# Score products of the first two batches in float32 from unsplit queries and keys

## The chip, the cores and the metric

The kernel runs on one core of one Trainium2 chip. The metric is device time in microseconds of one execution, lower is better. The core has TensorE (PE, with PEld for its weight loads), VectorE (DVE), ScalarE (ACT), GpSimd (POOL), and SyncE (SP), which here issues the transfers.

## The reference

Eight batches, eight heads, 576 positions, head width 64: block-causal attention (blocks of 64), then a feed-forward layer over all 4608 tokens.

```python
scores = scale * np.matmul(q, k.transpose(0, 1, 3, 2))
mask = block_i >= block_j
scores = np.where(mask, scores, -1000000000.0)
scores = scores - np.max(scores, axis=-1, keepdims=True)
attn = np.exp(scores)
attn = attn / (np.sum(attn, axis=-1, keepdims=True) + 1e-09)
out = np.matmul(attn, v)
...
h = x @ w_in
g = np.where(h >= 1, h, np.where(h <= -1, 0.0, (h + 1) ** 2 / 4))
return g @ w_out
```

All is float32, q and k of some size (standard deviation 0.8), so the products need more than one pass of a reduced format.

## The kernel before

Work goes by pairs of heads: 8 batches x 4 pairs = 32 pairs, the pairs of batch 0 first. `attention_steps` cuts each pair into eight steps and sets what the current pair, the next (its loads and turns) and the last (its product with the values) do in each. After 36 steps one step of `feed_forward` (twelve products of 512 columns) is written behind each attention step. Beside both runs `prepare_weights`, which splits the 64 pieces of the two weight matrices into high and low parts, by ACT, DVE, POOL, ACT and POOL in turn (L169 to L187), and has them done by about the end of batch 1. The framework then fixes each engine's order and the waits; each engine works strictly in that order.

A float32 product is made in one of two ways. *Split*: the operands become a high and a low part of type float32r, and the product is a sum of float32r matmuls. *Plain*: a matmul on float32 itself. Constants say which batches do what: `PLAIN = 2` (batches 0 and 1 multiply probabilities by values plainly), `RAW = 2` (from batch 2 on q and k are split after they are turned). In batches 0 and 1 q and k are split first: `split_q` (L351, L352) scales q and makes its parts on DVE; `split_k` makes k's high part on DVE (L363) and its low part on POOL (L364; for the very first pair on DVE).

The parts lie side by side, so that one turn (a matmul against the identity, L422) of a 128-token tile turns high and low at once: rows 0 to 63 one part, rows 64 to 127 the other. `turned` does four tiles of one head for q or k, copies the bank to `qb` or `kb` (L427, ACT), and has the upper or lower half moved to `qa` or `ka` by a transfer (L433; for the first head of the first pair by DVE, L429). `turned_last` does the same for the last 64 positions of both heads (L451, L456, L457).

`product` then makes a score tile of 128 queries from two float32r matmuls: L482 over `qa`, `ka` (68 rows: the high parts and four rows that hold the mask) and L485 over `qb`, `kb` (128 rows: the cross terms). `scores(j, g)` calls it for head j in three groups: tiles 0 and 1 (128 and 256 keys), tile 2 (384), tile 3 (512). `scores_last` takes the last 64 queries of both heads together as 128 columns, in two halves of 288 keys; `qa` and `qb` hold zeros beside each head's own 64 columns there, so the two heads' products are summed. After the product: maximum (L505, L529, DVE), exponential (L509, L535, ACT), reciprocal and scaling (L491, L492, L515, L541, DVE), turn of the probabilities (L554 in batch 0; in batch 1 by way of a transfer, L552), copy (L545, ACT), product with the values (L591). L541 runs once in a pair.

Of the kernel before, what the change touches and what calls it, by code (L numbers as in the profile page):

```python
# [8 lines left out]
F32 = mybir.dt.float32  # L9
# [3 lines left out]
AX = mybir.AxisListType  # L13
I32 = mybir.dt.int32
U32 = mybir.dt.uint32

# [7 lines left out]
def block_attn_then_ffn(  # L24
# [25 lines left out]
    G0 = 256  # L50
    G1 = S - G0
    SCALE = 1.0 / float(D) ** 0.5
# [39 lines left out]
    ident = ident_r.bitcast(F32)  # L92
# [28 lines left out]
    pcs = [const.tile([P, 2, BLK], F32R, tag=f"pcs{i}", name=f"pcs{i}") for i in range(2)]  # L121
# [16 lines left out]
    rows = mrow[:, :, :SM].rearrange("p s (t c) -> p s t c", c=P)  # L138
# [116 lines left out]
    class Pair:  # L255
# [4 lines left out]
        def __init__(self, b, hp):  # L260
            self.b, self.hp = b, hp

            self.plain = b < PLAIN
            self.first = b == 0 and hp == 0


            self.hop = b >= HOP
            self.raw = b >= RAW

            self.far = b >= FAR  # L270
            self.pr, self.nat = {}, {}
# [33 lines left out]
        def load(self, name):  # L305
            src = {"q": q, "k": k, "v": v}[name]
            h0 = 2 * self.hp
            if name == "v" and self.plain:

                self.vs = []  # L310
                both = att1.tile([P, 2, NTL + 1, 2, D], F32, tag="pb1", name="vs")
                for j in range(2):
                    vs = both[:, j]
                    nc.gpsimd.memset(vs[:, :, 1 - j, :], 0.0)
                    nc.sync.dma_start(
                        vs[:, :NTL, j, :], src[self.b, h0 + j, :SM, :].rearrange("(t p) d -> p t d", p=P)
                    )
                    nc.sync.dma_start(vs[:BLK, NTL, j, :], src[self.b, h0 + j, SM:, :])
                    self.vs.append(vs)
                return  # L320
            t_ = att2.tile([P, 2 * NTL + 2, D], F32, tag="nat", name=name + "n")
            if name == "v":
                for j in range(2):
                    nc.sync.dma_start(
                        t_[:, j * NTL : (j + 1) * NTL, :],
                        src[self.b, h0 + j, :SM, :].rearrange("(t p) d -> p t d", p=P),
                    )
                nc.sync.dma_start(
                    t_[:BLK, 2 * NTL :, :],
                    src[self.b, h0 : h0 + 2, SM:, :].rearrange("h p d -> p h d"),  # L330
                )
            else:

                nc.sync.dma_start(
                    t_[:, : 2 * NTL, :].rearrange("p (h t) d -> p h (t d)", h=2),
                    src[self.b, h0 : h0 + 2, :SM, :].rearrange("h (p t) d -> p h (t d)", t=NTL),
                )
                for j in range(2):
                    nc.sync.dma_start(
                        t_[j * BLK : (j + 1) * BLK, 2 * NTL, :], src[self.b, h0 + j, SM:, :]  # L340
                    )
            self.nat[name] = t_

        def split_q(self):
            if self.raw:
                return

            qn = self.nat.pop("q")[:, : 2 * NTL + 1, :]
            self.qs = att1.tile([P, 2 * NTL + 1, 2, D], F32R, tag="qs", name="qs")
            for c0, c1 in ((0, 2 * NTL), (2 * NTL, 2 * NTL + 1)):  # L350
                nc.vector.tensor_scalar_mul(self.qs[:, c0:c1, 0, :], qn[:, c0:c1, :], SCALE)  # L351
            nc.vector.scalar_tensor_tensor(  # L352
                out=self.qs[:, :, 1, :], in0=qn, scalar=SCALE,
                in1=self.qs[:, :, 0, :].bitcast(F32), op0=ALU.mult, op1=ALU.subtract,
            )

        def split_k(self):
            if self.raw:
                return
            kn = self.nat.pop("k")[:, : 2 * NTL + 1, :]  # L360
            self.ks = att1.tile([P, 2 * NTL + 1, 2, D], F32R, tag="ks", name="ks")
            for c0, c1 in ((0, 2 * NTL), (2 * NTL, 2 * NTL + 1)):
                nc.vector.tensor_copy(self.ks[:, c0:c1, 1, :], kn[:, c0:c1, :])  # L363
            (nc.vector if self.first else nc.gpsimd).tensor_tensor(  # L364
                out=self.ks[:, :, 0, :], in0=kn, in1=self.ks[:, :, 1, :].bitcast(F32),
                op=ALU.subtract,
            )
# [29 lines left out]
        def turned_raw(self, j):  # L397
# [10 lines left out]
            for a, bt, hi0 in ((qa, qb, 0), (ka, kb, D)):  # L408
                nc.sync.dma_start(
                    a[:D, j, :SM].bitcast(F32), bt[hi0 : hi0 + D, j, :SM].bitcast(F32)  # L410
                )

        def turned(self, is_q, j):

            if self.raw:
                if is_q:
                    self.turned_raw(j)
                return
            src, a, bt, hi0 = (self.qs, qa, qb, 0) if is_q else (self.ks, ka, kb, D)
            ps = work_bank("ps_qk")  # L420
            for t in range(NTL):
                nc.tensor.transpose(  # L422
                    ps[:, t * P : (t + 1) * P].bitcast(F32R), src[:, j * NTL + t, :, :], ident_r
                )

            turned = ps[:, :SM].rearrange("p (t c) -> p c t", t=NTL)
            nc.scalar.copy(bt[:, j, :SM].rearrange("p (c t) -> p c t", t=NTL), turned)  # L427
# [9 lines left out]
        def turned_last(self):  # L437

            ps = work_bank("ps_qk")
            if self.raw:  # L440
                ps = ps[:, :P]
                nc.tensor.transpose(ps.bitcast(F32R), self.qk[:, 2 * NTL, :, :], ident_r)
                ps = ps.rearrange("p (h c) -> p h c", h=2)
                self.parted(last_blocks, ps)
                for i, a in enumerate((qa, ka)):
                    nc.vector.tensor_scalar_mul(
                        last_blocks(a)[:D], ps[i * D : (i + 1) * D], 1.0 if i else SCALE
                    )
                return
            for i, src in enumerate((self.qs, self.ks)):  # L450
                nc.tensor.transpose(  # L451
                    ps[:, i * P : (i + 1) * P].bitcast(F32R), src[:, 2 * NTL, :, :], ident_r
                )
            for i, (a, bt, hi0) in enumerate(((qa, qb, 0), (ka, kb, D))):
                blocks = ps[:, i * P : (i + 1) * P].rearrange("p (h c) -> p h c", h=2)
                nc.scalar.copy(last_blocks(bt), blocks)  # L456
                nc.vector.tensor_copy(last_blocks(a)[:D], blocks[hi0 : hi0 + D])  # L457
# [14 lines left out]
        def begin_b(self):  # L472
            dt, n = (F32, 1) if self.plain else (F32R, 2)
            self.pb = [att1.tile([P, 2, NTL, G1], dt, tag=f"pb{i}", name=f"pb{i}") for i in range(n)]
            self.pc = (
                [att1.tile([BLK, 2, BLK], dt, tag="pa01", name="pc")] if self.plain else pcs
            )
            if not self.plain:
                self.x32 = att1.tile([P, S], F32, tag="x32", name="x32")

        def product(self, ps, j, c0, k0, n, first, last):
            nc.tensor.matmul(  # L482
                ps, qa[:KA, j, c0 : c0 + P], ka[:KA, j, k0 : k0 + n], start=first, stop=False
            )
# [400 lines left out]
```

## Time and profile before

| what | number |
|---|---|
| median of 3 runs | 1267.78 us (1264.84 to 1269.26) |
| profiled execution | 1269.69 us, span 1267.9 us |
| L541 (one in each pair) | first at 25.8 us, last at 1058.7 us |
| transfers, whole span | 215.43 MB, mean 170 GB/s |

Shares of the whole span mix three stages: batch 0 with attention alone, batch 1 with attention, feed-forward and the weights' split, and the rest. The prediction therefore reads the profile by stretches of the span.

### The profile page before, as it was taken

What the parts mean: (1) busy time and instruction counts of PE and PEld (TensorE: products, weight loads), DVE (VectorE), ACT (ScalarE), POOL (GpSimd) and SP (SyncE); (2) the same over time, 40 slices, a digit from 0 to 9 for tenths busy, and PEclk for the clock granted to TensorE, in tenths of its full rate; (3) what the DMA queues carried; (4) which work ended last, traced back from release to release, by engine and by line L of the source; (5) the groups of instructions that cost most, each with busy time, mean ns of one, the idle gap of its engine ahead of it and who ended that gap; (6) DMA issues with size and microseconds to landing.
All of it is one profiled execution on the core that took longest, in us unless ns stands there. A gap on an engine that the chain in (4) does not pass through costs nothing.

```text
span 1267.9 us, 20253 instructions
## 1 busy us (share of the span) xinstructions
PE 1200.1 (95%) x6280; PEld 998.8 (79%) x6280; DVE 887.0 (70%) x2188; ACT 703.2 (55%) x1827; POOL 394.6 (31%) x430
## 2 busy tenths in 40 slices
PE   5888889899999999999999999999999999999998
PEld 4666667678888888888888888888888888888886
DVE  8898877758777777777777777787777777322222
ACT  5787656646566655665656655566556555222222
POOL 3555655522222222222222222222222222222222
PEclk9888988999999999999999999999999999999999
DMA  5566666667888655555554655465556433422432
GB/s 158 167 176 215 203 228 197 217 198 237 260 273 266 215 162 158 154 175 163 156 162 145 187 157 152 138 189 153 160 154 190 137 128 118 132 87 98 133 100 100
DMA packets 185259, 215.43 MB, mean 170 GB/s; under 512 B 113840, under 2 KB 132272, under 8 KB 184384
## 3 DMA queue, kind: packets, MB, share of 16 engines
q1 hardware_dynamic: 185152, 214.14, 54.9%
q8 instruction: 50, 0.82, 0.3%
q14 instruction: 57, 0.47, 0.1%
HBM read 134.74 MB, written 31.98 MB: 131 GB/s over the span
## 4 chain that ended last, share of the span: by engine, by line
PE 69%; DVE 16%; ACT 6%; issue 5%; DMA 1%; POOL 1%; SPq 1%; ACTq 0%; POOLq 0%; DVEq 0%
PE ph L770 29%; PE po L794 15%; PE po L799 7%; PE ps_av L591 7%; PE ps_s L482 4%; ACT pr L509 3%; PE ps_s L485 3%; DVE t L780 2%; PE ps_t L552 2%; DVE t L783 2%; ACT t L779 2%; DVE pb L547 2%; DVE nm L505 2%; DVE sm L491 1%; DVE pr L515 1%
## 5 line engine op out<-in xcount | busy, mean ns | idle before, releaser
L785 POOL TENSOR_TENSOR gl<-t,gh 128x512 fp32r<-128x512 f32 x144 | 187.5, 1302 | 510.2 <-ACT gh L784 333.2
L794 PE MATMUL po<-wo,gh 128*128 128x512 f32 x1152 | 296.1, 397 | 0.5 <-DMA wo<-wo_split 0.3
L794 PEld LDWEIGHTS po<-wo,gh 128*128 128x128 f32 x1152 | 212.5, 189 | 44.5 <-DMA wo<-wo_split 0.7
L770 PE MATMUL ph<-xh,wih 128*128 128x512 f32 x576 | 232.9, 404 | 1.6 <-DVE t L783 1.6
L770 PE MATMUL ph<-xh,wil 128*128 128x512 f32 x576 | 228.8, 397 | 0.0
L770 PE MATMUL ph<-xl,wih 128*128 128x512 f32 x576 | 227.8, 396 | 0.5 <-DVE xl L627 0.5
L780 DVE SCALAR_TENSOR_TENSOR t<-t 128x512 f32<-128x512 f32 x144 | 101.5, 705 | 168.0 <-ACT t L779 165.2
L779 ACT ACTIVATE t<-ph 128x512 f32<-128x512 f32 x144 | 85.9, 597 | 173.8 <-PE ph L770 173.8
L509 ACT ACTIVATE pr<-ps_s,nm 128x128 f32<-128x128 f32 (+3 forms) x256 | 134.1, 527 | 60.5 <-DVE nm L505 58.4
L784 ACT CAST gh<-t 128x512 fp32r<-128x512 f32 x144 | 89.5, 621 | 120.3 <-DVE t L783 120.0
L799 PE MATMUL po<-wo,gl 128*128 128x512 f32 x576 | 155.6, 392 | 0.0
L482 PE MATMUL ps_s<-ka,qa 68*128 68x288 f32 (+4 forms) x384 | 135.3, 367 | 15.0 <-ACT pr L509 5.4
L379 POOL TENSOR_TENSOR vsr<-vn,vsr 128x256 fp32r<-128x256 f32 (+1 forms) x96 | 55.2, 576 | 246.2 <-ACT vsr L378 244.6
L770 PEld LDWEIGHTS ph<-xh,wil 128*128 128x128 f32 x576 | 109.5, 190 | 23.8
L770 PEld LDWEIGHTS ph<-xh,wih 128*128 128x128 f32 x576 | 109.8, 191 | 21.7 <-DVE t L783 2.3
L799 PEld LDWEIGHTS po<-wo,gl 128*128 128x128 f32 x576 | 108.7, 189 | 23.1
L505 DVE TENSOR_REDUCE nm<-ps_s 128x1 f32<-128x128 f32 (+3 forms) x256 | 118.8, 482 | 10.4 <-PE ps_s L485 9.4
L770 PEld LDWEIGHTS ph<-xl,wih 128*128 128x128 f32 x576 | 109.7, 190 | 20.5 <-DVE xl L627 0.9
L485 PE MATMUL ps_s<-kb,qb 128*128 128x288 f32 (+4 forms) x384 | 121.1, 322 | 0.0
L515 DVE TENSOR_SCALAR pr<-pr,sm 128x128 f32<-128x128 f32 (+3 forms) x256 | 107.3, 440 | 5.4
L783 DVE TENSOR_TENSOR t<-ph,t 128x512 f32<-128x512 f32 x144 | 98.7, 686 | 2.2
L491 DVE TENSOR_SCALAR sm<-sm 128x1 f32<-128x1 f32 (+1 forms) x224 | 52.0, 232 | 68.3 <-ACT pr L509 65.7
(111 smaller groups left out, 1871.4 us busy)
## 6 DMA issues: line engine op xcount, KB each, us to landing
wo<-wo_split SPq DMA_DIRECT2D x144, 512.0 KB, 3.5
prr<-pr SPq DMA_DIRECT2D x96, 192.0 KB, 2.5
prr<-pr SPq DMA_DIRECT2D x72, 256.0 KB, 2.8
out_dram<-ob SPq DMA_DIRECT2D x36, 256.0 KB, 2.9
bits<-in_moe_w_in_dram SPq DMA_DIRECT2D x32, 256.0 KB, 3.5
bits<-in_moe_w_out_dram SPq DMA_DIRECT2D x32, 256.0 KB, 3.0
wo_split<-ws SPq DMA_DIRECT2D x16, 512.0 KB, 2.9
qa<-qb SPq DMA_DIRECT2D x63, 128.0 KB, 2.4
```

Source lines behind the costliest of these rows:

```text
L482: nc.tensor.matmul(ps, qa[:KA, j, c0 : c0 + P], ka[:KA, j, k0 : k0 + n], start=first, stop=False)
L485: nc.tensor.matmul(ps, qb[:, j, c0 : c0 + P], kb[:, j, k0 : k0 + n], start=False, stop=last)
L505: nc.vector.tensor_reduce(out=nm[:, i : i + 1], in_=ps[:, cs], axis=AX.X, op=ALU.max, negate=True)
L509: nc.scalar.activation(pr[:, cs], ps[:, cs], AF.Exp, bias=nm[:, i : i + 1], scale=1.0, accum_out=sm[:, i : i + 1],)
L515: nc.vector.tensor_scalar_mul(pr[:, cs], pr[:, cs], sm[:, i : i + 1])
L770: nc.tensor.matmul(ph, w[:, cc, fs], x[:, cc, xs], start=(cc == 0 and i == 0), stop=(cc == NCC - 1 and i == 2),)
L779: nc.scalar.activation(t_, ph, AF.Relu, bias=0.5, scale=0.5)
L780: nc.vector.scalar_tensor_tensor(out=t_, in0=t_, scalar=1.0, in1=t_, op0=ALU.min, op1=ALU.mult)
L783: nc.vector.tensor_tensor(out=t_, in0=ph, in1=t_, op=ALU.max)
L785: nc.gpsimd.tensor_tensor(out=gl, in0=t_, in1=gh.bitcast(F32), op=ALU.subtract)
L794: nc.tensor.matmul(po[tt], gh[:, ts_], wo[:, w, :], start=(fc == 0 and w == 0), stop=False)
L799: nc.tensor.matmul(po[tt], gl[:, ts_], wo[:, 0, :], start=False, stop=fc == NFC - 1)
```

## The change

`UNSPLIT = 2`: the pairs of batches 0 and 1 skip `split_q` and `split_k`. The two heads' q (or k) are loaded so that tile t holds both heads' 64 numbers side by side, and `turned_unsplit` turns four such tiles (float32) for both heads at once: head 0 in rows 0 to 63, head 1 in rows 64 to 127. One ACT instruction copies the bank out (with the scale, for q) into a tile `qkt` that holds turned q and k of a pair; two buffers alternate. `turned_last_unsplit` turns the last blocks and writes q's to the diagonal of `diag`, a 128x128 part of a constant tile `corner` that is zero beside its two blocks.

`product` becomes, for a tile of one head, one float32 matmul over that head's 64 rows, and one float32r matmul over the four mask rows (rows 64 to 67 of `qa` and `ka`), which touches only the last 128 columns. For the last block it is one float32 matmul over 128 rows for both heads. A float32 matmul stands once in the order and runs as two instructions on PE.

```diff
+    UNSPLIT = 2
+    corner = att1.tile([P, G0 + P], F32, tag="pa01", name="corner")
+    nc.vector.memset(corner[:, P:], 0.0)
...
         def split_q(self):
-            if self.raw:
+            if self.raw or self.unsplit:
                 return
...
+        def turned_unsplit(self, is_q):
+            if is_q:
+                tag = ("qs", "ks")[self.hp % 2]
+                both = att1.tile([P, 2, S], F32, tag=tag, name="qkt")
+                self.qt, self.kt = both[:, 0, :], both[:, 1, :]
+                self.diag = corner[:, (1 + self.hp % 2) * P :][:, :P]
+            src = self.nat["q" if is_q else "k"]
+            ps = work_bank("ps_qk")
+            for t in range(NTL):
+                nc.tensor.transpose(ps[:, t * P : (t + 1) * P], src[:, 2 * t : 2 * t + 2, :], ident)
+            nc.scalar.mul(
+                (self.qt if is_q else self.kt)[:, :SM].rearrange("p (c t) -> p c t", t=NTL),
+                ps[:, :SM].rearrange("p (t c) -> p c t", t=NTL), SCALE if is_q else 1.0,
+            )
+
+        def turned_last_unsplit(self):
+            ps = work_bank("ps_qk")
+            for i, name in enumerate("qk"):
+                nc.tensor.transpose(
+                    ps[:, i * BLK : (i + 1) * BLK], self.nat.pop(name)[:BLK, 2 * NTL :, :],
+                    ident[:BLK, :BLK],
+                )
+            for j in range(2):
+                rows = slice(j * D, (j + 1) * D)
+                nc.scalar.mul(self.diag[rows, rows], ps[rows, :BLK], SCALE)
+            nc.scalar.copy(self.kt[:, SM:S], ps[:, BLK : 2 * BLK])
...
         def product(self, ps, j, c0, k0, n, first, last):
+            if self.unsplit and c0 == SM:
+                if j == 0:
+                    nc.tensor.matmul(ps, self.diag, self.kt[:, k0 : k0 + n], start=True, stop=True)
+                return
+            if self.unsplit:
+                rows = slice(j * D, (j + 1) * D)
+                nc.tensor.matmul(
+                    ps, self.qt[rows, c0 : c0 + P], self.kt[rows, k0 : k0 + n],
+                    start=first, stop=False,
+                )
+                nc.tensor.matmul(
+                    ps[:, n - P :], qa[D:KA, j, c0 : c0 + P], ka[D:KA, j, c0 : c0 + P],
+                    start=False, stop=last,
+                )
+                return
```

What it does to the order of the engines. PE in batch 1, head 1's first two groups; before, each tile is two float32r products, with a turn of the next pair's keys between:

```order
L482 MATMUL ps_s<-ka,qa 128x128
L485 MATMUL ps_s<-kb,qb 128x128
L482 MATMUL ps_s<-ka,qa 128x256
L485 MATMUL ps_s<-kb,qb 128x256
L422 MATMUL ps_qk<-ident_r,ks 128x128 x4
L552 MATMUL ps_t<-ident_r,vsr_111 128x128 x4
L794 MATMUL po<-wo,gh 128x512 x8
L799 MATMUL po<-wo,gl 128x512 x4
L482 MATMUL ps_s<-ka,qa 128x384
L485 MATMUL ps_s<-kb,qb 128x384
```

The same place after the change (L544 is the float32 product over 64 rows, L548 the mask product over four):

```order
L544 MATMUL ps_s<-qkt 128x128
L548 MATMUL ps_s<-ka,qa 128x128
L544 MATMUL ps_s<-qkt 128x256
L548 MATMUL ps_s<-ka,qa 128x128
L623 MATMUL ps_t<-ident_r,vsr_111 128x128 x4
L865 MATMUL po<-wo,gh 128x512 x8
L870 MATMUL po<-wo,gl 128x512 x4
L544 MATMUL ps_s<-qkt 128x384
L548 MATMUL ps_s<-ka,qa 128x128
```

Product and mask now alternate, and the second turn of the keys is gone. DVE at the same pair, before: the split of the next pair's q and k stands among the scaling of the probabilities.

```order
L505 TENSOR_REDUCE nm<-ps_s 128x1
L351 TENSOR_SCALAR qs<-qn 128x8x64
L491 TENSOR_SCALAR sm<-sm 128x2
L351 TENSOR_SCALAR qs<-qn 128x64
L492 RECIPROCAL sm<-sm 128x2
L363 CAST ks<-kn 128x8x64
L515 TENSOR_SCALAR pr<-pr,sm 128x128
L515 TENSOR_SCALAR pr<-pr,sm 128x256
L491 TENSOR_SCALAR sm<-sm 128x1
L457 CAST qa<-ps_qk 64x2x64
L492 RECIPROCAL sm<-sm 128x1
L352 SCALAR_TENSOR_TENSOR qs<-qn,qs 128x9x64
```

After (L562, L563 and L586 are the old L491, L492 and L515; L576 is L505, and L177 to L183 are the weights' split):

```order
L562 TENSOR_SCALAR sm<-sm 128x2
L563 RECIPROCAL sm<-sm 128x2
L586 TENSOR_SCALAR pr<-pr,sm 128x128
L586 TENSOR_SCALAR pr<-pr,sm 128x256
L576 TENSOR_REDUCE nm<-ps_s 128x1
L177 TENSOR_SCALAR work<-work 128x256
L180 TENSOR_SCALAR work<-work 128x256
L183 SCALAR_TENSOR_TENSOR work<-work 128x256
L562 TENSOR_SCALAR sm<-sm 128x1
L563 RECIPROCAL sm<-sm 128x1
```

The five instructions of the split and the copy of the last block are gone from between. On PE the last block's products, before:

```order
L482 MATMUL ps_s<-ka,qa 128x288
L485 MATMUL ps_s<-kb,qb 128x288
L482 MATMUL ps_s<-ka,qa 128x288
L485 MATMUL ps_s<-kb,qb 128x288
L482 MATMUL ps_s<-ka,qa 128x288
L485 MATMUL ps_s<-kb,qb 128x288
L482 MATMUL ps_s<-ka,qa 128x288
L485 MATMUL ps_s<-kb,qb 128x288
L552 MATMUL ps_t<-ident_r,prs 128x128 x3
```

After, with the work around it:

```order
L544 MATMUL ps_s<-qkt 128x512
L548 MATMUL ps_s<-ka,qa 128x128
L623 MATMUL ps_t<-ident_r,vsr_112 128x128 x3
L865 MATMUL po<-wo,gh 128x512 x8
L870 MATMUL po<-wo,gl 128x512 x4
L540 MATMUL ps_s<-qkt,corner 128x288 x2
L623 MATMUL ps_t<-ident_r,prs 128x128 x3
```

Eight products became two.

More of the change, by code (lines that the diff above doesn't have):

```diff
@@ L332, in load @@
             else:
[L334 to L338, printed above, removed]
+                if self.unsplit:
+                    for j in range(2):
+                        nc.sync.dma_start(
+                            t_[:, j : 2 * NTL : 2, :],
+                            src[self.b, h0 + j, :SM, :].rearrange("(p t) d -> p t d", t=NTL),
+                        )
+                else:
                     nc.sync.dma_start(
-                        t_[j * BLK : (j + 1) * BLK, 2 * NTL, :], src[self.b, h0 + j, SM:, :]
-                    )
+                        t_[:, : 2 * NTL, :].rearrange("p (h t) d -> p h (t d)", h=2),
+                        src[self.b, h0 : h0 + 2, :SM, :].rearrange("h (p t) d -> p h (t d)", t=NTL),
+                    )
+                if self.unsplit:
+                    nc.sync.dma_start(
+                        t_[:BLK, 2 * NTL :, :],
+                        src[self.b, h0 : h0 + 2, SM:, :].rearrange("h p d -> p h d"),
+                    )
+                else:
+                    for j in range(2):
+                        nc.sync.dma_start(
+                            t_[j * BLK : (j + 1) * BLK, 2 * NTL, :], src[self.b, h0 + j, SM:, :]
+                        )
             self.nat[name] = t_
         def split_q(self):
-            if self.raw:
+            if self.raw or self.unsplit:
                 return
@@ L411, in turned_raw @@
                 )
+        def turned_unsplit(self, is_q):
[18 more added lines that the diff above has]
+                    ident[:BLK, :BLK],
+                )
+            for j in range(2):
+                rows = slice(j * D, (j + 1) * D)
+                nc.scalar.mul(self.diag[rows, rows], ps[rows, :BLK], SCALE)
+            nc.scalar.copy(self.kt[:, SM:S], ps[:, BLK : 2 * BLK])
         def turned(self, is_q, j):
+            if self.unsplit:
+                if j == 0:
+                    self.turned_unsplit(is_q)
+                return
             if self.raw:
@@ L437, in turned_last @@
         def turned_last(self):
+            if self.unsplit:
+                self.turned_last_unsplit()
+                return
             ps = work_bank("ps_qk")
@@ L475, in begin_b @@
             self.pc = (
-                [att1.tile([BLK, 2, BLK], dt, tag="pa01", name="pc")] if self.plain else pcs
+                [corner[:BLK, :P].rearrange("p (h c) -> p h c", h=2)] if self.plain else pcs
             )
```

9 lines of the change are left out of this document (8 added, 1 removed).

## The prediction

> **What bounds the kernel now.** First the first part of the page, then the table of windows, cut where the change's eight pairs (batches 0 and 1) begin and end. The columns after the length are busy microseconds, with instruction counts in brackets; then come the granted TensorE clock, the DMA share and GB/s.
>
> ```profile
> PE 1200.1 (95%) x6280; PEld 998.8 (79%) x6280; DVE 887.0 (70%) x2188; ACT 703.2 (55%) x1827; POOL 394.6 (31%) x430
> 0.00:25.80 25.80, 12.36 (x54) 10.14 (x54) 21.22 (x67) 14.16 (x41) 9.54 (x18) 1.00 0.57 159
> 25.80:114.60 88.80, 72.96 (x390) 58.65 (x391) 80.14 (x250) 69.78 (x213) 46.81 (x60) 0.90 0.61 179
> 114.60:290.10 175.50, 156.16 (x730) 121.87 (x729) 127.19 (x309) 101.93 (x284) 85.12 (x102) 0.92 0.67 211
> 25.80:290.10 264.30, 229.12 (x1119) 180.51 (x1120) 207.33 (x558) 171.71 (x496) 131.93 (x161) 0.92 0.65 201
> 290.10:323.30 33.20, 32.80 (x184) 27.70 (x183) 26.42 (x65) 20.87 (x54) 9.14 (x10) 1.00 0.70 211
> ```
>
> The cuts are the starts of the L541 instruction, one in each pair. From 290 us on PE is busy 32.80 of 33.20 us and nothing there is changed: that stage only shifts. From 25.8 to 114.6 (batch 0) VectorE is busy 80.14 of 88.80 us and PE 72.96; from 114.6 to 290.1 (batch 1 with the first feed-forward steps) PE is busy 156.16 of 175.50 and VectorE 127.19. So before 290 us there are two near-bounds, VectorE first and then PE, and the change moves work from the one to the other. PE is idle 264.30 - 229.12 = 35.2 us in the two stages together. What ends that idle time stands in the waits of that stretch (total, times, longest):
>
> ```profile
> PE ps_t L554 <- DVE sm L491: 7.5, 3, 3.8
> PE ps_s L482 <- ACT kb L427: 4.1, 2, 3.7
> PE ps_av L591 <- ACT pr L509: 3.7, 3, 2.2
> PE ps_t L554 <- DVE pr L515: 3.4, 4, 1.5
> PE ph L770 <- DVE t L783: 1.6, 3, 0.7
> ```
>
> Of the 35.2 us, 7.5 + 3.4 + 1.6 = 12.5 us end with VectorE and 4.1 us with the copy of keys that the change replaces: 16.6 us that lighter VectorE and ScalarE queues could return. The rest ends with exponentials, transfers and copies that stay.
>
> **The change, part by part.** Instructions that go, with mean ns in the same stretch:
>
> ```profile
> L364 POOL TENSOR_TENSOR ks<-kn,ks 128x576 fp32r<-128x576 f32 x6 | 8.6, 1435 | 0.6 <-DVE ks L363 0.3
> L427 ACT CAST kb<-ps_qk 128x512 fp32r<-128x512 f32 x14 | 8.2, 585 | 0.0
> L352 DVE SCALAR_TENSOR_TENSOR qs<-qn,qs 128x576 fp32r<-128x576 f32 x6 | 4.4, 739 | 0.0
> L363 DVE CAST ks<-kn 128x512 fp32r<-128x512 f32 x6 | 3.3, 551 | 0.0
> L351 DVE TENSOR_SCALAR qs<-qn 128x512 fp32r<-128x512 f32 x6 | 2.9, 480 | 0.0
> L363 DVE CAST ks<-kn 128x64 fp32r<-128x64 f32 x6 | 2.5, 409 | 1.2 <-DMA kn<-in_k_dram 1.2
> L457 DVE CAST ka<-ps_qk 64x128 fp32r<-64x128 f32 x7 | 2.1, 293 | 0.2
> L351 DVE TENSOR_SCALAR qs<-qn 128x64 fp32r<-128x64 f32 x6 | 2.0, 338 | 0.0
> L457 DVE CAST qa<-ps_qk 64x128 fp32r<-64x128 f32 x7 | 1.9, 272 | 0.0
> L456 ACT CAST qb<-ps_qk 128x128 fp32r<-128x128 f32 x7 | 1.9, 272 | 0.0
> ```
>
> VectorE loses 739 + 551 + 480 + 409 + 293 + 338 + 272 = 3082 ns a pair. POOL loses 1.4 us a pair. ScalarE goes from four wide copies and two of the last block (4 x 585 + 2 x 272 = 2.9 us) to two wide and three of the last block (2 x 585 + 3 x at most 272 = 2.0 us): 0.9 us less, nothing of it on PE's own path beyond the 4.1 us of waiting above. Four transfers a pair go; the loads are cut in other pieces:
>
> ```profile
> ka<-kb SPq DMA_DIRECT2D x63, 128.0 KB, 2.3
> qn<-in_q_dram SPq DMA_DIRECT2D x8, 256.0 KB, 3.5
> vs<-in_v_dram SPq DMA_DIRECT2D x16, 128.0 KB, 2.3
> ```
>
> A query or key load of 256 KB (3.5 us to landing) becomes two of 128 KB in 64-number pieces, the form of the value load, which lands in 2.3 us; the issues of a pair stay six, since the two last-block loads become one. They are issued a pair ahead, so I cost them at nothing; what covers them is that pair's 20 us. If a key load waits for its buffer, now held until the last block is turned, the transfers queued behind it on SP wait too: bound 0 to 2.3 us a pair, taken 0 because the last block is turned two steps before the next load is issued.
>
> PE pays. Its price per column comes from the order of time (start, length, group), batch 0's second pair and the end of batch 1:
>
> ```profile
> 33.26 0.31 PE L482 MATMUL ps_s<-ka,qa 68*128 68x128 f32 x1
> ...
> 33.80 0.60 PE L554 MATMUL ps_t<-ident_r,pr 128*128 128x128 f32 x4
> 34.15 0.42 PE L482 MATMUL ps_s<-ka,qa 68*128 68x384 f32 x1
> ...
> 34.59 0.23 PE L451 MATMUL ps_qk<-ident_r,qs 128*128 128x128 f32 x1
> ...
> 39.68 0.50 PE L482 MATMUL ps_s<-ka,qa 68*128 68x512 f32 x1
> ...
> 40.25 0.49 PE L554 MATMUL ps_t<-ident_r,pr 128*128 128x128 f32 x3
> ...
> 41.58 0.40 PE L482 MATMUL ps_s<-ka,qa 68*128 68x288 f32 x1 [0.27 <-DVE ka L457]
> ...
> 42.22 0.49 PE L554 MATMUL ps_t<-ident_r,pr 128*128 128x128 f32 x3
> 43.57 0.54 PE L422 MATMUL ps_qk<-ident_r,qs 128*128 128x128 f32 x4 [0.40 <-DVE xl L627]
> 43.95 0.46 PE L770 MATMUL ph<-xh,wih 128*128 128x512 f32 x1
> ...
> 277.30 0.43 PE L591 MATMUL ps_av<-pc,vs 64*128 64x64 f32 x2
> 277.66 2.21 PE L591 MATMUL ps_av<-pb,vs 128*128 128x320 f32 x8
> 279.80 0.43 PE L591 MATMUL ps_av<-pc,vs 64*128 64x64 f32 x2
> ```
>
> Products before, by distances of starts: 0.54 + 0.44 + 0.57 us for a head's three groups, and 0.64 us for four products of the last block, of which there are eight: 2 x 1.55 + 2 x 0.64 = 4.4 us a pair.
>
> A float32 product is two instructions on PE (the L591 group shows eight for four matmuls). From 277.66 to 279.80, 6 x 320 + 2 x 192 = 2304 columns and one change of rows (128 to 64) take 2.14 us; from 277.30 to 277.66, 2 x 64 columns and one change back take 0.36 us. Solved: 0.82 ns a column and 0.25 us a change of rows. The turns of L554, 0.11 us each within their group of four, say 0.86 ns a column and then 0.16 us a change. I take 0.82 ns and 0.20 us.
>
> After: 2 x 1280 + 2 x 288 = 3136 columns, twice 0.82 ns each, is 5.1 us; eight mask products of 128 columns, at the 0.64 us / (4 x 288) = 0.56 ns a column of the last block's old products, add 0.6 us. That is 5.7, so +1.3 us. Turns: sixteen at 0.095 us (0.38 us for four at 43.57) become eight at 0.11: -0.6 us.
>
> Changes of rows have no counterpart in the old products, all of which use 68 or 128 rows. Now a group goes 128 rows, 64 (product), 4 (mask), and for the first group 64 and 4 once more: 5 + 3 + 3 = 11 a head, 22 a pair, and one at the turn of the last block: 23. For head 0 the product uses rows 0 to 63 and the mask rows 64 to 67, so five of the 23 are between rows that do not overlap; the trace shows no such pair. I count half of them: 20.5, about 4.0 us at 0.20 us. The ends are none at all (0) and 23 x 0.25 = 5.75 us.
>
> The Trainium skill has a rule for either end. "TensorEngine Tiling (Array Packing)", Key Properties, says that a change of tiling mode drains the engine, which would charge all 23 (about 0.5 us a pair more than I take, +4 us in all); "TensorE: Matmul & The Clock Gate", Step-by-step, says that weights load ahead of a running matmul where the row groups do not conflict, which would charge 18 (-4 us in all). The row at 277.30 bears out the first for overlapping rows; no row decides for disjoint ones.
>
> PE in sum: +1.3 - 0.6 + 4.0 = +4.7 us a pair (ends +0.7 and +6.4). Between 25.8 and 290 us lie seven and a half pairs' scores: +35 us (ends +5 and +48). Against it:
> - Idle of PE: VectorE sheds 7.5 x 3.08 = 23 us, more than the 16.6 us of waits found above. I take 16 (ends 5 and 23).
> - Clock: 0.92 granted over 264.30 us is 21 us lost at most; the loss follows idle stretches, and PE grows denser. I take half, 10 (ends 0 and 18).
> - Start: the first pair's split and copy by VectorE go, of which these two rows lie on the chain of waits,
>
> ```profile
> 9.19 3.02 DMA ka<-mrow
> 22.23 1.28 DVE qs L352
> ```
>
> while the mask rows (landing at 12.21 us) are still needed, one memset more (of the new constant tile) heads VectorE's queue, and PE has more to do. I take -2 (ends -4 and +3).
>
> 35 - 16 - 10 - 2 = +7 us. The profiled execution took 1269.69 us (span 1267.9), 1.9 above the median of the runs shown, 1267.78; the forecast goes from the median: 1275.
>
> **Rivals.** *The clock returns more.* Denser PE work keeps the full clock nearly throughout, 18 us instead of 10: -1, so 1267. For it: 0.90 and 0.92 granted against 1.00 after 290 us. Against it: the waits on L509 remain, and they make the idle stretches. The same page's Part 1 says that idle windows of about 3.4 us halve the clock and busy ones restore it.
>
> *Faster.* The changes of rows are hidden and VectorE was the true bound: +5 - 12 - 2 = -9, so 1259. It decides if a product followed by its mask takes less than 0.1 us beyond its columns. Against it: the 0.36 us for two 64-column instructions.
>
> *PE takes it all.* Idle time comes from the softmax's own latency and stays: 35 - 5 - 3 = +27, so 1295. For it: PE 156.16 of 175.50 in batch 1.
>
> **How the numbers follow.** Forecast 0.40, clock 0.25, faster 0.23, PE takes it all 0.12. Slower by over 0.3% (3.8 us, about what a measurement tells from no change) is 0.52, within 0.25, faster 0.23. The range, 1258 to 1292, cuts the far parts of the second and third rival; the forecast's own range is 1271 to 1283.
>
> **What would show it.** Right: VectorE some 3 us a pair lighter before 290 us, the score products at about 9 to 10 us of PE a pair, about 0.2 us from each product's end to its mask, fewer waits on VectorE, pairs of batch 1 no shorter, and 33.2 us a pair unchanged afterwards. Wrong: a mask product that follows its product at once, a shorter batch 0, or a granted clock near 1.00 before 290 us.

## Result and the profile after

| | before | changed |
|---|---|---|
| median | 1267.16 us (1264.84 to 1269.26, 4 runs) | 1284.29 us (1281.31 to 1288.57, 4 runs) |
| profiled execution | 1269.69 us, span 1267.9 | 1283.15 us, span 1281.4 |

The ratio is 1.0138, with an interval of 1.0118 to 1.0158: slower, by 17 us where +7 was forecast. The new number is inside the range given, but not inside the forecast's own range of 1271 to 1283. The two profiled executions differ by 13.5 us; the rest lies between single executions, and no profile shows it.

The first part of the page and the table of windows of the changed kernel, cut as before at the start of the instruction that opens each pair (L541 is now L612). The columns are busy microseconds of PE, PEld, DVE, ACT and POOL with counts, then granted clock, DMA share, GB/s:

```profile
PE 1239.4 (97%) x6248; PEld 999.7 (78%) x6248; DVE 865.6 (68%) x2130; ACT 699.3 (55%) x1819; POOL 379.6 (30%) x423
0.00:27.70 27.70, 18.93 (x49) 10.64 (x49) 14.48 (x52) 13.09 (x39) 6.96 (x17) 1.00 0.54 147
27.70:130.30 102.60, 96.83 (x366) 62.08 (x367) 74.18 (x227) 68.19 (x212) 38.69 (x58) 0.82 0.55 164
130.30:303.50 173.20, 165.05 (x728) 118.80 (x727) 119.08 (x290) 100.75 (x280) 80.44 (x98) 0.97 0.71 225
27.70:303.50 275.80, 261.88 (x1092) 180.88 (x1093) 193.26 (x516) 168.93 (x490) 119.14 (x155) 0.91 0.65 202
303.50:336.70 33.20, 32.84 (x185) 27.76 (x183) 26.45 (x66) 20.87 (x54) 9.16 (x10) 1.00 0.87 279
```

The start grew by 1.9 us (25.8 to 27.7), batch 0 from 88.8 to 102.6 us (+13.8), batch 1 went from 175.5 to 173.2 (-2.3), and a later pair still takes 33.20 us. In sum +13.4 us, which is the difference of the two profiled executions (13.5). So the loss sits in batch 0. There PE's busy time went from 72.96 to 96.83 us while its granted clock (the share of full speed that TensorE is allowed) fell, by the rows, from 0.90 to 0.82. VectorE, near-bound before, is busy 74.18 of 102.60 us.

PE's idle time in both batches is 275.80 - 261.88 = 13.9 us, where it was 35.2. Its largest waits there (total, times, longest):

```profile
PE ps_av L662 <- ACT pr L580: 4.0, 3, 2.3
PE ps_t L625 <- DVE pr L586: 3.7, 2, 2.1
PE ps_qk L444 <- ACT pb L616: 2.4, 2, 2.0
PE ps_t L625 <- ACT pr L580: 1.6, 1, 1.6
```

The 7.5 us on VectorE's `sm` and the 4.1 us on the copy of keys are gone.

**A blind spot of the clock column.** The profile's record of the clock begins at 32.8 us in the kernel before and at 26.5 us in the changed one; ahead of it the column prints 1.00. The spacing of the products says otherwise. The same five turns of the probabilities, kernel before (at 26.40 us), then changed (at 28.79 us):

```profile
26.40 1.30 PE L554 MATMUL ps_t<-ident_r,pr 128*128 128x128 f32 x5 [2.08 <-DVE sm L491]
```

```profile
28.79 0.74 PE L625 MATMUL ps_t<-ident_r,pr 128*128 128x128 f32 x5 [1.61 <-ACT pr L580]
```

They start 0.213 us apart in the first and 0.109 us apart in the second. So the kernel before runs at half clock from its start until 32.8 us, 7.0 us of which belong to batch 0, and the 1.00 of both kernels' first row is no measurement. With those 7.0 us counted, batch 0's clock before the change is 0.86, not 0.90. In what follows half clock is counted with them.

What the forecast had not seen is in the windows at half clock. First two rows of the changed kernel's batch 0, then one of the kernel before:

```profile
29.90:47.00 17.10, 17.10 (x43) 10.42 (x42) 10.27 (x32) 10.28 (x33) 5.88 (x8) 0.50 0.37 117
77.70:87.90 10.20, 10.20 (x32) 6.51 (x31) 5.07 (x19) 6.05 (x18) 0.73 (x1) 0.50 0.42 117
```

```profile
49.80:56.60 6.80, 6.24 (x26) 5.47 (x26) 6.07 (x19) 3.72 (x10) 4.07 (x5) 0.50 0.54 149
```

Before, no recorded stretch at half clock was longer than 6.8 us. After the change one lasts 17.1 us and two last 10.2, and in them PE is busy 17.10 of 17.10 and 10.20 of 10.20 us. In batch 0 half clock covers 37.5 us instead of 24.0; in batch 1 it is 10 us instead of 27. One profile is not exact here: in three traces of the kernel before (two with streams appended behind it, below) batch 0 has 22.5, 24.0 and 25.7 us, and both batches together 43, 51 and 59.

### The profile page after: what moved, and what is told of

Its sections match the earlier page's. It is cut to its first block, busy times and chain, and to the rows that moved or that the text cites. A ratio compares the mean times of both kernels' runs of the same rounds, so it can differ in the third digit from the quotient of the medians.

```text
span 1281.4 us, 20013 instructions
## 1 busy us (share of the span) xinstructions
PE 1239.4 (97%) x6248; PEld 999.7 (78%) x6248; DVE 865.6 (68%) x2130; ACT 699.3 (55%) x1819; POOL 379.6 (30%) x423
## 4 chain that ended last, share of the span: by engine, by line
PE 65%; DVE 9%; ACT 4%; issue 3%; POOL 0%; ACTq 0%; POOLq 0%
PE ph L841 27%; PE po L865 15%; PE po L870 7%; PE ps_av L662 6%; PE ps_s L553 3%; ACT pr L580 3%; PE ps_s L556 2%; PE ps_t L623 2%; DVE t L851 2%; DVE pb L618 2%; DVE t L854 2%; ACT t L850 2%; DVE sm L562 1%; PE ps_qk L421 1%; DVE x L685 1%
## 5 line engine op out<-in xcount | busy, mean ns | idle before, releaser
L841 PE MATMUL ph<-xh,wil 128*128 128x512 f32 x576 | 226.2, 393 | 0.0
L576 DVE TENSOR_REDUCE nm<-ps_s 128x1 f32<-128x128 f32 (+3 forms) x256 | 118.8, 482 | 24.2 <-PE ps_s L548 21.0
L399 POOL TENSOR_TENSOR vsr<-vn,vsr 64x64 fp32r<-64x64 f32 (+1 forms) x96 | 55.6, 579 | 249.2 <-ACT vsr L398 247.6
L586 DVE TENSOR_SCALAR pr<-pr,sm 128x128 f32<-128x128 f32 (+3 forms) x256 | 103.8, 426 | 6.3 <-DVE sm L563 0.3
L562 DVE TENSOR_SCALAR sm<-sm 128x1 f32<-128x1 f32 (+1 forms) x224 | 52.7, 235 | 79.6 <-ACT pr L580 76.7
L553 PE MATMUL ps_s<-ka,qa 68*128 68x288 f32 (+4 forms) x288 | 99.4, 360 | 5.3 <-ACT pr L580 5.3
L556 PE MATMUL ps_s<-kb,qb 128*128 128x288 f32 (+4 forms) x288 | 88.7, 315 | 0.0
```

What stands on the lines that cost most here:

```text
L553: nc.tensor.matmul(ps, qa[:KA, j, c0 : c0 + P], ka[:KA, j, k0 : k0 + n], start=first, stop=False)
L556: nc.tensor.matmul(ps, qb[:, j, c0 : c0 + P], kb[:, j, k0 : k0 + n], start=False, stop=last)
L576: nc.vector.tensor_reduce(out=nm[:, i : i + 1], in_=ps[:, cs], axis=AX.X, op=ALU.max, negate=True)
L586: nc.vector.tensor_scalar_mul(pr[:, cs], pr[:, cs], sm[:, i : i + 1])
L841: nc.tensor.matmul(ph, w[:, cc, fs], x[:, cc, xs], start=(cc == 0 and i == 0), stop=(cc == NCC - 1 and i == 2),)
```

## The experiments

Theory A: the clock gate (whatever grants TensorE full or half clock) weighs how many of the array's rows work, not only whether PE is busy, so products over 64 rows (and the masks over 4) leave batch 0 at half clock; batch 1 has the feed-forward's 128-row products in between. Theory B: only PE's longer path counts; half clock comes from idle time as before, and the loss is columns and changes of rows.

**All products over 128 rows, first form.** The turned queries of each head are written by ScalarE into a buffer whose other 64 rows are zero; keys keep both heads; the mask uses 68 rows. This kernel keeps the values in one lasting tile, so that the positions from 256 on in batches 0 and 1 are weighted with another pair's values; the amount of work is the same.

```
-  self.qt[rows, c0 : c0 + P], self.kt[rows, k0 : k0 + n]
+  self.qz[j][:, c0 : c0 + P], self.kt[:, k0 : k0 + n]
...
-  qa[D:KA, j, c0 : c0 + P], ka[D:KA, j, c0 : c0 + P]
+  qa[:KA, j, c0 : c0 + P], ka[:KA, j, c0 : c0 + P]
```

> The changed kernel with every score product and mask product of batches 0 and 1 over 68 or 128 rows: q is written into two zero-padded copies, one for each head, and the mask product takes 68 rows of which 64 are zero. The passes stay, the changes of rows go; ScalarE issues one more 64x512 copy a pair. Theory A (the clock follows how many rows of TensorE work): the half-clock stretch of 17 us in batch 0 goes, batch 0 gets some 12 us shorter by the clock and some 3.5 us a pair by the changes of rows; in all 1245 to 1257 us. Theory B (the price is the length of PE's work alone, and the half clock comes from idle stretches as before): the changes of rows save 7.5 x 3.5 = 26 us at most, half-clock time in batch 0 stays near 37 us: 1258 to 1266 us.

Measured 1267.47 us, ratio to before 0.9985 (0.9974 to 0.9996). Its batch 0:

```profile
26.40:108.90 82.50, 71.81 (x369) 53.14 (x369) 71.91 (x219) 69.24 (x214) 40.63 (x57) 0.98 0.71 208
```

82.5 us at a clock of 0.98: the whole loss of batch 0 is gone. The time as a whole missed both theories' ranges: batch 1 became 176.8 us long, with 23.9 us at half clock, where the changed kernel has 173.2 and 10. And rows and changes of rows were altered together, so runs that separate them follow.

**Mask over 68 rows alone**, the float32 products still over 64 (the second - and + line above).

> Only the mask product is over 68 rows (64 of them zero); the float32 products stay on 64 rows. Changes of rows fall from 23 to 17 a pair. Theory A: little change of the clock, since the 64-row products stay: about 9 us less than the changed kernel, 1275 us. Theory B: the same 9 us. More than that would say that it is the four-row product which holds the clock down.

Measured 1288.69 us, ratio 1.0128 (1.0086 to 1.0171): nothing was gained, where both theories had 9 us. In this trace the record begins only at 50.2 us and the spacing shows half clock until then, which makes 39.7 us in batch 0, about as much as in the changed kernel. A mask over more rows does not help while the product uses 64.

**One batch alone**, batch 1 (`self.unsplit = b == 1`), then batch 0 (`UNSPLIT = 1`).

> The change in batch 1 alone; batch 0 splits as before. Both theories: batch 0 as before the change; batch 1 2 us shorter, as the two traces have it: 1263 to 1267 us. Theory A expects no half-clock stretch over 7 us, since the feed-forward's 128-row products stand between.

> The change in batch 0 alone; batch 1 splits as before. Both theories: the loss of the change and 2 us more, 1282 to 1287 us, with a half-clock stretch of 10 us or more in batch 0 in which PE is not idle.

Batch 1 alone: 1267.28 us, 0.9985 (0.9973 to 0.9997). Batch 0 alone: 1285.15 us, 1.0127 (1.0102 to 1.0152). Batch 0's row in the second:

```profile
28.20:134.20 106.00, 97.22 (x375) 64.31 (x375) 77.20 (x239) 69.67 (x212) 43.38 (x60) 0.83 0.53 159
```

Here too the column misses the first part, up to 35.9 us; with it batch 0 has 44.6 us at half clock. The same code costs 16 us where attention stands alone and nothing where the feed-forward runs beside it. Extra columns and changes of rows are alike in both.

**Streams behind the kernel before.** 17 us and more of one kind of product at a time, each kind led by 44 products over 128 rows. Nothing of the kernel is altered.

```
+    for i in range(40):
+        nc.tensor.matmul(pa_, wf[:64, i % 4, :P], wf[:64, i % 4, 512:1024], start=True, stop=True)
...
+    warm(44)
...
+    for i in range(14):
+        nc.tensor.matmul(pb_, wf[:64, i % 4, :P], wf[:64, i % 4, 512:1024], start=True, stop=False)
+        nc.tensor.matmul(pb_[:, 384:], wih[64:68, i % 4, :P], wih[64:68, i % 4, :P], start=False, stop=True)
...
+    for i in range(80):
+        nc.tensor.matmul(pg_, wih[64:68, i % 4, :P], wih[64:68, i % 4, 512:1024], start=True, stop=True)
```

> The kernel before, with extra streams of TensorE work behind its last product, each some 17 us long without a wait inside and each led by 44 products of 128 rows x 512 columns (p: 64-row float32 512 columns x40; 64-row float32 512 columns with a 4-row mask of 128 columns behind each x14; 128-row float32 x40; float32 turns x160; float32r turns x200; 64-row float32r x80; 4-row float32r x80). The answer is the granted clock inside each stream, not the time of the run. Theory A (the gate weighs how many rows of the array work): 128-row stream 1.00 all through, 64-row streams and the 4-row stream fall to half clock after 3 to 7 us, product with mask too; turns of 128 rows open. Theory B (the gate counts only whether TensorE is busy, and batch 0's half clock comes from idle time): 1.00 in every stream.

The windows of six streams of this one execution, in order (the two at 0.50 are cut where half clock begins, 4.4 and 5.0 us into the stream): float32 over 64 rows; float32 over 64 rows with a 4-row mask behind each; float32 over 128 rows; float32 turns; float32r over 64 rows; float32r over 4 rows. The float32r turns, not shown, ran at 1.00 like the float32 ones.

```profile
1273.00:1303.70 30.70, 30.70 (x73) 13.14 (x71) 0.00 (x0) 0.00 (x0) 0.00 (x0) 1.00 0.00 1
1318.30:1343.70 25.40, 25.40 (x33) 8.06 (x31) 0.00 (x0) 0.00 (x0) 0.00 (x0) 0.50 0.00 0
1356.30:1390.20 33.90, 33.90 (x80) 15.01 (x79) 0.00 (x0) 0.00 (x0) 0.00 (x0) 1.00 0.00 0
1400.60:1418.00 17.40, 17.40 (x160) 17.35 (x159) 0.00 (x0) 0.00 (x0) 0.00 (x0) 1.00 0.01 2
1455.50:1473.80 18.30, 18.30 (x81) 14.61 (x80) 0.00 (x0) 0.00 (x0) 0.00 (x0) 1.00 0.00 1
1489.00:1514.20 25.20, 25.20 (x61) 18.98 (x59) 0.00 (x0) 0.00 (x0) 0.00 (x0) 0.50 0.00 1
```

Theory B falls: two streams without any idle time run at 0.50. Theory A in its first form falls too: 64-row products alone keep a full clock that they find. Only with the mask and its changes of rows behind each do they lose it.

The stretches at half clock within these kernels last 3.4, 6.8, 10.2 or 17.1 us (leaving out the first and the last of a kernel), multiples of 3.41 us. I therefore worked out, from the order of time, how much of the array is at work in each 3.41 us between the clock's possible steps, called *rows at work* below: the time in which products stream their columns, times rows / 128, as a share of the 3.41 us. In the masked stream this is 0.32 to 0.38, in the plain 64-row streams 0.47 to 0.50. In the changed kernel's 17.1 us it is 0.53, 0.59, 0.45, 0.71, and full clock comes after 0.89. So a full clock is lost after a stretch below some 0.4, and what ends a half clock must be another, higher bound.

**What restores the clock.** Streams that start at half clock (behind 40 products over 4 rows).

```
+    stream("s64", 70, 64)
+    stream("s64x3_128x1", 72, 64, 64, 64, 128)
+    stream("s64x1_128x1", 72, 64, 128)
+    stream("s64x1_128x3", 72, 64, 128, 128, 128)
+    stream("s64x1_128x7", 72, 64, 128, 128, 128, 128, 128, 128, 128)
+    stream("s128", 70, 128)
```

> The kernel before, with streams of float32r products of 512 columns behind its last product. Each is led by 44 products over 128 rows (full clock) and 40 over 4 rows (half clock, as in the earlier streams), and then follows without a pause: 64 rows x70; 64, 64, 64, 128 in turn x72 (0.62 of the rows at work); 64, 128 x72 (0.75); 64, 128, 128, 128 x72 (0.88); 64 and seven times 128 x72 (0.94); 128 x70. The answer is how long the half clock lasts in each. Theory A as it now stands, from the stretches of 3.41 us of the runs so far (a half clock ended after a stretch in which TensorE's time, weighted by the rows used, was 0.74 or more, and not below 0.73): 64-row stream and the 0.62 mix stay at half clock to their end, 0.88, 0.94 and 128 rows are at full clock after 4 to 8 us, 0.75 less its changes of rows stays at half. Theory B (the gate counts only that TensorE is busy): each stream at full clock after 4 to 8 us.

The six streams, again of one execution, in this order:

```profile
1286.70:1316.90 30.20, 30.20 (x72) 22.74 (x71) 0.00 (x0) 0.00 (x0) 0.00 (x0) 0.50 0.00 1
1341.50:1382.70 41.20, 41.20 (x73) 20.20 (x73) 0.00 (x0) 0.00 (x0) 0.00 (x0) 0.50 0.00 0
1407.20:1459.20 52.00, 52.00 (x74) 20.84 (x74) 0.00 (x0) 0.00 (x0) 0.00 (x0) 0.50 0.00 0
1486.70:1525.00 38.30, 38.30 (x73) 18.88 (x73) 0.00 (x0) 0.00 (x0) 0.00 (x0) 0.55 0.00 0
1549.90:1572.10 22.20, 22.20 (x73) 14.29 (x73) 0.00 (x0) 0.00 (x0) 0.00 (x0) 0.88 0.00 1
1596.20:1613.80 17.60, 17.60 (x71) 14.45 (x71) 0.00 (x0) 0.00 (x0) 0.00 (x0) 0.90 0.01 1
```

PE is busy in all of every one. The 64-row stream stays at half clock for its 30.2 us; the stream over 128 rows is released within 4 us. One expectation missed: the mix with three 128-row products in four was to be released in 4 to 8 us and stayed at half clock for 34.5 of its 38.3. With its changes of rows four of its products take 2.30 us, where their columns alone take 1.71, so its rows at work are 0.65 and not 0.88; the mix of one in eight, with 0.80, is released. The two pure streams are the clean pair: both stream without a pause, and only their rows differ.

The same sum over the twelve kernels without appended streams (20 to 330 us of each as far as the clock is recorded, at 0.83 ns a column for float32 and 0.42 for float32r, twice that at half clock) has 123 stretches at half clock. Of the 41 at 0.73 or less 39 were followed by half clock again, of the 21 between 0.74 and 0.80 17 by full clock, and so were all 61 above. Eleven of the 41 had PE streaming for 0.78 or more of the time, rows not counted, and stayed down all the same. Turns count as work here: a stretch of the wide run below (from 70.4 us) was released with 0.82 of rows at work, of which 0.60 were turns.

**128 rows in the kernel, values unaltered.** Queries go by two transfers a pair into zero-padded buffers; the mask goes over 68 rows in the first run (below) and over its 4 rows in the second (`D:KA` for `:KA`); in the third only batch 0 is widened.

```
+  self.qz = (qb, kb)[self.hp % 2].bitcast(F32)
+  for j in range(2):
+      rows = slice(j * D, (j + 1) * D)
+      nc.sync.dma_start(self.qz[rows, j, :SM], self.qt[rows, :SM])
...
+  nc.tensor.matmul(ps, self.qz[:, j, c0 : c0 + P], self.kt[:, k0 : k0 + n], start=first, stop=False)
+  nc.tensor.matmul(ps[:, n - P :], qa[:KA, j, c0 : c0 + P], ka[:KA, j, c0 : c0 + P], start=False, stop=last)
```

> The changed kernel, but the score products of both batches run over all 128 rows: the turned queries go by two transfers into buffers whose other head's half is zero, the keys keep both heads side by side, and the mask product runs over 68 rows (the first 64 zero). The values and all else as in the changed kernel; two transfers more a pair. Columns are the same, so a product costs the same time at full clock; 6 changes of rows fewer a head. Theory A: half clock before 290 us falls from some 57 us to 25 to 35 us, batch 0 ends at 105 to 115 us instead of 130, the whole 1262 to 1270. Theory B (longer path of TensorE alone, with the changes of rows its main price): changes of rows saved 6 x 0.2 us x 2 heads x 7.5 pairs = 10 to 18 us, clock as in the changed kernel, 1266 to 1275.

> As the run with both products over 128 and 68 rows, but the mask product stays on its 4 rows: the changes of rows stay (128 to 4 and back, two for every group), only the row count of the float32 products is doubled. Theory A: the clock comes back as in the wide run, and the changes cost 8 x 2 x 0.2 = 3 us a pair at most, so 1270 to 1285 with batch 0 at a granted clock over 0.90. Theory B: no better than the changed kernel, 1282 to 1289, batch 0's clock 0.80 to 0.84.

> The wide products in batch 0 alone; batch 1 has the 64-row products of the changed kernel, where its feed-forward steps add 128-row products. Theory A: batch 0 as in the wide run (ends at 105 to 115 us), batch 1 as in the changed kernel (173 us long) or up to 4 us longer: 1258 to 1270, the best of all. Theory B: between the wide run and the changed kernel, 1270 to 1282.

Measured 1266.26 us (0.9984, 0.9971 to 0.9996), 1271.27 us (1.0019, 1.0004 to 1.0034) and 1268.39 us (0.9994, 0.9979 to 1.0009). The first run (the *wide* run below) has a time that both theories allow, and 23.9 us at half clock, which only A does. Both batches together, of the first and the second run:

```profile
25.90:287.00 261.10, 230.06 (x1095) 175.12 (x1093) 191.39 (x512) 167.54 (x491) 120.58 (x154) 0.95 0.69 208
```

```profile
29.40:293.40 264.00, 245.31 (x1099) 176.86 (x1098) 192.64 (x512) 167.82 (x492) 120.09 (x154) 0.95 0.68 205
```

With the changes of rows around the mask left in (second run) and the float32 product's row count doubled, half clock from batch 0's start on falls from 47.8 to 23.9 us, and the median by 13 us to a value that theory A allowed and B did not. Of the 261.88 - 245.31 = 16.6 us of PE time saved, 12 are the clock (half of 23.9 us). The rest fits the changes between 128 and 64 rows, six a pair, which go as well, so theory B has some 4 us of the 16.6. Taking the changes of rows around the mask out too saves 5 us more of time and 15 us of PE, most of which turns into idle time (31.0 us against 18.7). Widening batch 0 alone was expected to be the best and is not: a miss, though its interval overlaps the first run's, so the two aren't told apart. Its batch 0 is the same code as the first run's, and has 20.5 us at half clock against 13.6: a difference of some 7 us between two profiles tells nothing.

The order of time shows what a change of rows costs. A 128-column product, its mask and what follows: changed kernel, then the second run, both at full clock.

```profile
62.11 0.48 PE L544 MATMUL ps_s<-qkt 64*128 64x128 f32 x2
62.52 0.32 PE L548 MATMUL ps_s<-ka,qa 4*128 4x128 f32 x1
62.77 0.70 PE L544 MATMUL ps_s<-qkt 64*128 64x256 f32 x2
63.40 0.32 PE L548 MATMUL ps_s<-ka,qa 4*128 4x128 f32 x1
```

```profile
58.76 0.39 PE L555 MATMUL ps_s<-qkt,qb 128*128 128x128 f32 x2
59.07 0.32 PE L559 MATMUL ps_s<-ka,qa 4*128 4x128 f32 x1
59.32 0.70 PE L555 MATMUL ps_s<-qkt,qb 128*128 128x256 f32 x2
59.95 0.32 PE L559 MATMUL ps_s<-ka,qa 4*128 4x128 f32 x1
```

A float32 product is two passes, and two passes of 128 columns are 0.21 us. From 62.11 to 62.52 is 0.41, so 0.20 us beyond the columns: half of it because the second pass starts 0.1 us late just behind a change of rows, half for the change to the mask. From 62.52 to 62.77 is 0.25 where the mask's columns are 0.05: 0.20 again. In the second run the product at 58.76 stands behind work over 128 rows, no change leads it, and its distance is 0.31. The product at 59.32 stands behind the mask, and takes 0.63 to the next mask, as over 64 rows (62.77 to 63.40).

**Unread work in PE's wait**, of 128 rows and (second run, `ident_r[:4]`) of 4, on the wide kernel:

```
+            if self.b == 0 and (j, g) == (0, 2):
+                for _ in range(12):
+                    nc.tensor.matmul(ps[:, :P], ident_r[:128], ident_r[:128], start=True, stop=True)
```

> The wide kernel of both batches with twelve products of 128 rows x 128 columns that nobody reads, ahead of the turns of head 0's last group in each pair of batch 0, where TensorE waited 0.7, 2.3, 3.3 and 1.9 us for VectorE in the wide run. Theory A: stretches that held 0.14 to 0.24 of row-weighted work get about 0.35 more, the three half-clock stretches of batch 0 (3.4 + 3.4 + 6.8 us) go or shrink, batch 0 shorter by 0 to 5 us: 1260 to 1267. Theory B (idle time alone): the same, since the products fill idle time too. The next run tells the two apart.

> As the run before, but the twelve unread products use 4 rows instead of 128: TensorE is as busy, the array is not. Theory A: half clock in batch 0 as in the wide run (10 to 17 us), and the filling costs its own time where the wait is shorter: 1265 to 1271. Theory B: as with 128 rows, 1260 to 1267.

Measured 1268.35 us (1.0012, 0.9998 to 1.0025) and 1268.83 us (1.0010, 0.9998 to 1.0023). Neither theory's gain appeared: batch 0 became 95.1 and 96.7 us long instead of 87.8 and batch 1 some 6 us shorter (both together 262.7 and 264.0 us against 261.1), and the 128-row filling left 13.6 us at half clock in batch 0, as much as without it. Waits moved to other places, so this pair decides nothing.

**Useful work in the same wait**: the next pair's query turns ahead of that wait instead of behind it.

```
                 cur.scores(1, 0)
+                if nxt:
+                    nxt.turned(True, 0)
                 cur.turn(0, 2)
-            if nxt:
+            if nxt and cur.far:
                 nxt.turned(True, 0)
```

`cur.far` is false in both batches, so the order is another in batch 1 too.

> The wide kernel of both batches, with one step written in another order in batch 0: the next pair's query turns (four, 0.11 us each at full clock) and their copy by ScalarE come ahead of the turns of head 0's last group, for which TensorE waited 0.7 to 3.3 us in each pair of the wide run, instead of behind them. Nothing is added. Theory A: the wait shrinks by the turns' 0.4 to 0.9 us, and the stretches that held 0.14 to 0.24 of row-weighted work rise to 0.3 or so, too little to keep the clock: 1263 to 1267, batch 0 at 84 to 89 us. Theory B (each piece of idle time removed also removes half clock): 1258 to 1263.

Measured 1264.58 us, 0.9968 (0.9957 to 0.9979): the lowest of all, 19.7 us below the changed kernel, though its interval still touches the wide run's.

```profile
25.70:110.70 85.00, 72.80 (x364) 53.68 (x365) 71.89 (x216) 66.17 (x208) 37.35 (x55) 0.94 0.63 185
```

Batch 0 is 85.0 us long against 87.8 in the wide run, as theory A had it; batch 1 is 174.8 against 173.3. Half clock is 10.2 us against 13.6 in batch 0 and 27.3 against 23.9 in both, no more than two profiles of one code differ.

## Why the prediction was right in parts and wrong in sum

- **PE's price** (+4.7 us a pair, +35 us): held. PE's busy time in the two batches grew by 261.88 - 229.12 = 32.8 us. The part of it at half clock is 46.8 us in both kernels, so the growth is work: 4.4 us a pair.
- **Changes of rows** (0.20 us each, half of those between rows that don't overlap): the size held, the half did not. In all 13 cases at full clock the mask starts 0.201 or 0.202 us after the last pass of a 128-column product; 0.107 of that are the pass's columns, so 0.094 are this change. The work behind a mask starts 0.20 us late, and a second pass just behind a change 0.107. By these distances a pair's changes cost some 3.8 us, where 4.0 was taken. The 13 cases take in both heads, head 0's disjoint rows too. In "TensorEngine Tiling (Array Packing)", Key Properties, the Trainium skill says that a change of mode drains the engine; the trace agrees in that no change is free, and shows no discount.
- **Idle time** (-16 us): right in kind, a little small: 35.2 to 13.9 us, -21. The waits named for it, on `sm` and on the copied keys, are those that went.
- **VectorE** (3.1 us a pair lighter): 887.0 to 865.6 us over the span is 21.4, or 2.7 for each of eight pairs. PE's waits on it in batch 0 fell from 12.8 to 4.5 us.
- **Start** (-2 us): +1.9. PE is busy 18.93 us there instead of 12.36, and this outweighs the shorter split. The prediction took the first row's 1.00 for full clock; both kernels are at half clock nearly throughout it, where each added float32 pass costs double.
- **Clock** (-10 us): **the step that failed.** It came out at about 0: PE is busy for 46.8 us at half clock in both kernels, which is 23.4 us lost before and after (19 to 25 in the three traces of the kernel before). "The loss follows idle stretches, and PE grows denser" is half a rule. In batch 1 it held: 27 us of half clock became 10. In batch 0 idle time also fell, from 15.8 to 5.8 us, yet half clock went from 24.0 to 37.5 us. There a clock that has fallen to half returns only after a stretch of 3.4 us with some three quarters of the rows at work, and 64-row products cannot give that however dense they stand.

Put together, 33 - 21 + 0 + 2 = +14, where the two profiles differ by 13.4 between the cuts. This sum closes by the way its terms are counted and is no check of them. The misses on idle time (5 us more won than forecast) and on the start (4 us more lost) cancel by luck; what is left of the miss is the clock.

The page "TensorE: Matmul & The Clock Gate", Part 1, of the Trainium skill says that about 3.4 us of sustained activity restore the full clock; the rival "the clock returns more" leaned on it. The runs agree for 128 rows and disagree for 64: 30.2 us without a gap at 0.50. This was the largest thing missed.

Of the signs named beforehand, the lighter VectorE, the fewer waits on it, score products at about 9 us of PE a pair (by the distances above, at full clock) and the unchanged 33.2 us came true. The mask stands 0.2 us beyond the columns of its product, as named, but half of that lies between the product's two passes. Batch 1 got 2.3 us shorter, where no shortening was expected. Of the rivals "PE takes it all" (1295) came nearest in time, but by the wrong mechanism: idle time did not stay, and the clock in batch 0 took the gain.

The profile before could hardly show that rows count: its score products use 68 or 128 rows, and 64 rows stand only in a few short instructions.

What stays open: the exact bound that ends a half clock. By sums that rest on the columns alone it lies between 0.73 and 0.80 of rows at work, but the stream of one 64-row product in four was released after 34.5 us behind a stretch with 0.69, like those before it. Open too is why 26 of 49 stretches at full clock between 0.30 and 0.40 lost it and 23 did not. Whether turns alone restore it was not run.

## What to carry to other kernels

When a change swaps full-height products for ones over fewer rows, cost the clock by rows at work and not by busy time: a busy PE at half height can stay at half clock for as long as nothing taller comes between. Padding the contraction with zeros to 128 rows adds no column and here bought some 13 us; padding the small added product as well, so that it follows without a change of rows, bought 5 us more. Check a clock column against the spacing of equal products before you trust its 1.00. When two bounds lie close together, look at what the first one's relief does to the second one's clock, stage by stage.

## What the hardware showed unexpectedly

- The granted clock depends on rows at work. Falling: of 57 stretches of 3.41 us at full clock with under 0.30, 54 lost it, and of the 828 with 0.40 or more none did. Rising takes 0.74 to 0.80.
- A stream over 64 rows keeps a full clock (float32 for 30.7 us, float32r for 18.3, both at 1.00), but the one that started at half clock (float32r) stayed there for 30.2 us. With a 128-column mask over 4 rows behind each 512 columns the float32 stream loses a full clock while PE is never idle.
- Just behind a change of rows the second pass of a float32 product starts 0.1 us late, over 64 rows and over 128 alike: 0.41 us to what follows two passes of 128 columns, against 0.31 where no change leads.
